# A wait that ties each group of GpSimd's operations to the VectorE instruction before it in the plan

## The chip, the cores and the metric

The kernel runs on one core of one Trainium2 chip. The core has five instruction streams that run side by side and meet only at semaphores: TensorE (PE), VectorE (DVE), ScalarE (ACT), GpSimd (POOL) and SyncE (SP), which only issues DMAs here. The metric is the device time of one execution in microseconds, the median of several.

## What is computed

Three blocks follow each other, for a batch of 8 sequences of 576 rows and 512 columns, all in float32:

```python
def sm_attn(qq, kk, vv):
    s = scale * np.matmul(qq, kk.transpose(0, 1, 3, 2))
    s = s - np.max(s, axis=-1, keepdims=True)
    a = np.exp(s)
    a = a / (np.sum(a, axis=-1, keepdims=True) + 1e-09)
    return np.matmul(a, vv)
p_packed = sm_attn(p, k, v)              # 32 packed rows for each head
out = sm_attn(q, p_packed, p_packed)     # 8 heads of 64
...
h = np.maximum(x @ w_in, 0.0)            # second block
u, v = (h[..., :d_ff // 2], h[..., d_ff // 2:])
v_n = (v - mu) / np.sqrt(var + 1e-06)
v_s = np.einsum('ts,bsd->btd', w_spatial, v_n) + b_spatial[None, :, None]
gated = u * v_s
return (gated @ w_out).astype(np.float32)
...
theta = x @ w_theta                      # third block
zr, zi = x * np.cos(theta), x * np.sin(theta)
y = np.einsum('ts,bsd->btd', w_tok_r, zr) + np.einsum('ts,bsd->btd', w_tok_i, zi)
u = x + y
return (u + np.maximum(u @ w_ch, 0.0)).astype(np.float32)
```

## The kernel before, in words

The matmuls run in fp32r, a float32 of shortened mantissa. To keep the precision, most operands are split into a high part and the rest: ScalarE writes the high part (`hi`, line 263) and VectorE or GpSimd subtracts it from the value (`lo`, line 266); a product is then three matmuls, high by high, high by low and low by high. These subtractions are the greater part of what GpSimd does. The rest is subtraction and multiplication in the softmax (lines 549 and 560), the products x cos and x sin in `rotate` (line 1226), differences of blocks in `TTop` (line 1392), and some sums of weight blocks.

No loop over tiles is written out in the order in which it runs. The source adds tasks to a planner (`Plan.add`): an engine or a choice of engines, an estimated duration, a function that emits the instructions, a due key, and what the task reads, writes and newly allocates. A task is one group of instructions on one engine. `Plan.run` then goes through time: of all ready tasks it takes the one that can start first, with a preference for the lowest key within 0.25 us, fixes its engine and its buffers, and emits it. So the order on each engine is the plan's order. A hand-tuned table (`SHIFT`) moves the keys of single tasks.

Tasks marked `port=True` are those of VectorE and GpSimd that work from SBUF to SBUF. The planner lets only one of these run at a time on the two engines together: the variable `port` is the end of the last one. That is a rule of the plan alone. In the program, an instruction waits for the data that it reads and for the buffers that it writes, by semaphores, and for nothing else (`manual_schedule`). Two instructions of VectorE and GpSimd that share no data may come in the other order, or at once.

The stages in time: up to about 330 us the eight batches pass through attention (`first`, `second` with its softmax in `second_quad`, tiles `t`, `sm`, `at`), the input matrix (`m_part`, `v_part`, `u_part`, tiles `vf`, `VN`, `VA`) and the spatial matmul (`g_part`, tile `gs`), while the weights of the third block are read, converted from 64-bit words (`cvt_tasks`, lines 705 to 714, tiles `raw`, `cvg`) and split. From about 330 us on come the products with the combined weights (`x_tile`, `x_pair`, tiles `WX`, `gp`, `xs`, `fa`), `rotate`, the splits into `op`, the token mixing (`product`, tiles `wg`, `WR`) in a scheme with sums and differences of blocks, the additions into `xs` (lines 1273, 1278), and the channel matmul (`chan`, line 1354) with the store of the result. `xs` and `fa` are the two results of a tile; `bank` is a PSUM bank.

Of the kernel before, what the change touches and what calls it, by code (L numbers as in the profile page):

```python
# [116 lines left out]
class Res:  # L117


    def __init__(self, t=None, pool=None):  # L120
        self.t, self.pool = t, pool
        self.before, self.writers, self.readers, self.left, self.end = [], [], [], 0, 0.0
# [36 lines left out]
class Plan:  # L159
# [5 lines left out]

    OVERLAP = {"DVE": 0.07, "ACT": 0.09}

    def __init__(self):
        self.tasks, self.pools = [], {}
        self.group = 0  # L170
        self.lag = 0.0
# [33 lines left out]
    def run(self):  # L205
        free = {}
        port = pipe = 0.0
        ready = [t for t in self.tasks if not t.wait]
        log = []
        n = len(self.tasks)  # L210
        while ready:
            by = {}
            for t in ready:
                s = self.start_of(t)
                if s is not None:
                    for e in t.choice:
                        by.setdefault(e, []).append((max(s, free.get(e, 0.0), port if t.port and e != "ACT" else 0.0), t))
            pick = None
            for e, c in by.items():
                m = min(s for s, _ in c)  # L220
                s, t = min(((s, t) for s, t in c if s <= m + self.SLACK), key=lambda x: (x[1].key, x[0]))
                if pick is None or s < pick[0]:
                    pick = s, t, e
            assert pick, "no buffer comes free"
            s, t, t.eng = pick
            t.dur = t.choice[t.eng]
            ready.remove(t)
            for x in t.new:
                p = self.pools[x.pool]
                best = min(range(len(p)), key=lambda i: p[i][0])  # L230
                x.t = p.pop(best)[1]
            free[t.eng] = s + t.dur - self.OVERLAP.get(t.eng, 0.0)
            end = s + t.dur
            if t.size:
                pipe = max(s + 0.3, pipe) + t.size / self.BYTES_PER_US
                end = pipe + 2.0
            if t.port and t.eng != "ACT":
                port = end
            t.fn(t.eng) if t.told else t.fn()
            n -= 1  # L240
            log.append((s, end, t))
            for x in t.res:
                x.left -= 1
                x.end = max(x.end, end)
                if not x.left and x.pool:
                    self.pools[x.pool].append((x.end, x.t))
            for u in t.users:
                u.ready = max(u.ready, end + ((0.0 if t.eng == "PE" else 0.05) if t.eng in u.choice and len(u.choice) == 1 else 0.3 if t.eng == "PE" else 0.2) + (u.lag if t.eng != "PE" else 0.0))
                u.wait -= 1
                if not u.wait:  # L250
                    ready.append(u)
        assert not n
        self.log = log


@with_exitstack
def moe_kernel(ctx: ExitStack, tc, qT, kT, v, pT, w_in, wsT, bs, w_out,
               w_theta, wrT, wiT, w_ch, out):
    nc = tc.nc
    V, A, G, PE, SP = nc.vector, nc.scalar, nc.gpsimd, nc.tensor, nc.sync  # L260

    def hi(out, in_):
        A.activation(out=out, in_=in_, func=AF.Copy)  # L263
# [69 lines left out]
    M = [apm.tile([128, 2, DFF], F32R, name=f"M{i}") for i in range(2)]  # L333
    AT = [apm.tile([128, 2, 640], F32R, name=f"at{i}") for i in range(2)]

    P = Plan()

    def tiles(pool, name, n, shape, dtype=F32):
        P.pool(name, [pool.tile(shape, dtype, name=f"{name}{i}") for i in range(n)])

# [44 lines left out]
    def load(key, dst, pairs, size, r=(), w=(), new=()):  # L385
        def fn():
            for o, i in pairs():
                SP.dma_start(out=o, in_=i)
        P.add("SP", 0.6 * len(pairs()) if not new else 0.6, fn, key, r=r, w=w, new=new, size=size)

# [13 lines left out]
    def rows(r):  # L404
        return slice(r * 64, r * 64 + 64)

    def logits(key, stat, stat_r, x, new, s, one):

        for quads in ((0,), (1,)) if one else ((0, 1),):
            def f(quads=quads):  # L410
                heads_mm(lambda q, c: s[q][c].t[:, :CH], lambda q, j, r: stat[rows(r), q, j * 32:j * 32 + 32],
                         lambda q, j, r, c: x[q].t[rows(r), j, c * CH:(c + 1) * CH], quads)
            P.add("PE", 1.0, f, key + 3 * quads[0], r=[y for q in quads for y in (stat_r[q], x[q])],
                  new=[y for q in quads for y in (*s[q], *new[q])])

    def banks(n):

        return [[P.res("bank") for _ in range(2)] for _ in range(n)]


    def first(b, key):
        kt, vr = ([P.res(n) for _ in range(2)] for n in ("kt", "vr"))
        s = banks(2)

        def load_p():
            SP.dma_start(out=pk[b % 2].rearrange("p q n -> p (q n)"), in_=pT[:, b * 128:(b + 1) * 128])
        P.add("SP", 0.6, load_p, key - 6.2, w=[R_pk[b % 2]], size=65e3)
        for q in range(2):
            def load_k(q=q):
                SP.dma_start(out=kt[q].t, in_=kT[b, q * 256:(q + 1) * 256, :].rearrange("(j p) t -> p j t", p=128))  # L430
            P.add("SP", 0.6, load_k, key - 6, new=[kt[q]], size=590e3)
        for q in range(2):
            def load_v(q=q):
                c = slice(q * 256, (q + 1) * 256)
                SP.dma_start(out=vr[q].t[:, 0:4, :], in_=v[b, 0:512, c].rearrange("(j p) t -> p j t", p=128))
                SP.dma_start(out=vr[q].t[0:64, 4, :], in_=v[b, 512:576, c])
            P.add("SP", 1.1, load_v, key - 4 + q, new=[vr[q]], size=590e3)
        logits(key, pk[b % 2], [R_pk[b % 2]] * 2, kt, [[], []], s, not b)
        for q in range(2):
            first_quad(b, q, key + 4 * q, s[q], vr[q])  # L440
# [565 lines left out]
    early = {*R_pk, *R_PP.values(), *R_win}  # L1006
    late = {*R_at.values(), *R_M.values()}
# [9 lines left out]
    made = {}  # L1017
# [546 lines left out]
```

## Time and profile before

| | us |
|---|---|
| median of 3 runs | 849.61 (848.97 to 850.67) |
| the profiled execution | 851.74 |
| its span, first to last instruction | 850.0 |
| PE busy in it | 833.3 |
| VectorE busy | 614.6 |
| ScalarE busy | 459.5 |
| GpSimd busy | 320.1 |

The busy time of an engine is the union of its instructions' times in the span. Ends of matmuls are modelled, so a busy PE is not PE at its peak. The 1.7 us between the profiled execution's time and its span lie before the first and after the last instruction. The mean granted clock of TensorE is 0.998 of full speed.

### The profile page before, as it was taken

The numbers are of one execution on the slowest core, as the hardware profiler recorded it, in microseconds if no ns is written. First come the engines' busy times: TensorE is split into PE (matmuls) and PEld (weight loads), VectorE is DVE, ScalarE is ACT, GpSimd is POOL, SyncE is SP. The second block draws the span as 40 slices with busy tenths as digits, with TensorE's granted clock in tenths as the row PEclk, the third lists the DMA queues.
The fourth block names the chain that finished last, engine by engine and source line by source line (L and its number), as shares of the span: only waits on it lengthen the run. The fifth ranks groups of instructions, "written<-read, shape, count | busy, mean of one in ns | idle before, by whom it ended". The sixth has DMA issues, their size and how long they took to land.

```text
span 850.0 us, 14886 instructions
## 1 busy us (share of the span) xinstructions
PE 833.3 (98%) x5526; PEld 690.4 (81%) x5526; DVE 614.6 (72%) x1187; ACT 459.5 (54%) x963; POOL 320.1 (38%) x243
## 2 busy tenths in 40 slices
PE   9999999999999999989999999999999999999998
PEld 7868888887787899868778888888887888888886
DVE  5999989888778983675985678775579675556333
ACT  4786856765675763673464564344553454534310
POOL 1312414233624043034256552515554221655520
PEclk9999999999999999999999999999999999999999
DMA  9986666647564239361133224142331343322621
GB/s 333 317 284 230 188 191 201 231 128 214 160 203 117 83 97 275 87 221 54 51 120 114 85 75 130 52 154 84 92 110 60 102 118 107 85 76 62 182 67 62
DMA packets 86860, 119.04 MB, mean 140 GB/s; under 512 B 10882, under 2 KB 57730, under 8 KB 86788
## 3 DMA queue, kind: packets, MB, share of 16 engines
q1 hardware_dynamic: 86788, 118.09, 44.4%
q8 instruction: 43, 0.70, 0.4%
q14 instruction: 29, 0.24, 0.1%
HBM read 88.38 MB, written 29.69 MB: 139 GB/s over the span
## 4 chain that ended last, share of the span: by engine, by line
PE 83%; DVE 11%; DMA 3%; ACT 1%; issue 1%; POOL 0%; SPq 0%; POOLq 0%; DVEq 0%; ACTq 0%
PE bank L269 80%; PE bank L1328 2%; DMA kt<-kT 1%; DMA raw<-wrT 1%; DVE fa L1226 1%; PE bank L461 1%; DVE op L266 1%; DVE fa L1392 1%; DMA vr<-vL 1%; DVE xs L1278 0%; DVE gp L266 0%; DVE sm L554 0%; DVE one L447 0%; DVE fa L1218 0%; DVE M L266 0%
## 5 line engine op out<-in xcount | busy, mean ns | idle before, releaser
L269 PE MATMUL bank<-op,wg 128*128 128x512 f32 x672 | 175.6, 395 | 1.0 <-DVE xs L1273 1.0
L269 PE MATMUL bank<-WX,gp 128*128 128x512 f32 x630 | 153.6, 391 | 2.0 <-ACT fa L1176 1.6
L269 PEld LDWEIGHTS bank<-op,wg 128*128 128x128 f32 x672 | 125.1, 189 | 26.9 <-DVE xs L1273 1.4
L269 PEld LDWEIGHTS bank<-WX,gp 128*128 128x128 f32 x630 | 117.7, 188 | 28.0 <-ACT fa L1176 2.5
L266 POOL TENSOR_TENSOR op<-fa,op 128x512 fp32r<-128x512 f32 x72 | 96.2, 1355 | 111.7 <-ACT op L263 109.8
L269 PE MATMUL bank<-WS,VN 128*128 128x288 f32 x768 | 116.4, 298 | 0.0
L269 PEld LDWEIGHTS bank<-WS,VN 128*128 128x128 f32 x768 | 105.8, 188 | 8.4 <-issue 4.5
L269 PE MATMUL bank<-WC,uT 128*128 128x512 f32 x432 | 103.9, 390 | 1.1 <-DVE xs L1354 1.1
L269 PEld LDWEIGHTS bank<-WC,uT 128*128 128x128 f32 x432 | 80.7, 188 | 18.1 <-DVE xs L1354 1.5
L1176 ACT ACTIVATE xs<-bank 128x256 f32<-128x256 f32 x60 | 22.9, 382 | 124.0 <-PE bank L269 118.0
L263 ACT ACTIVATE op<-fa 128x512 fp32r<-128x512 f32 x96 | 59.2, 630 | 55.0 <-PE bank L269 52.3
L1226 POOL TENSOR_TENSOR fa<-xs,fa 128x512 f32<-128x512 f32 x27 | 36.5, 1368 | 129.0 <-ACT fa L1222 103.9
L1273 DVE TENSOR_TENSOR xs<-bank,xs 128x512 f32<-128x512 f32 x56 | 37.9, 687 | 42.0 <-PE bank L269 41.9
L269 PE MATMUL bank<-M,at 128*128 128x512 f32 x240 | 59.6, 397 | 0.0
L1354 DVE SCALAR_TENSOR_TENSOR xs<-bank,xs 128x512 f32<-128x512 f32 (+1 forms) x37 | 24.9, 674 | 43.9 <-PE bank L269 43.8
L269 PE MATMUL bank<-at,M 128*128 128x288 f32 x384 | 54.6, 298 | 0.1
L269 PEld LDWEIGHTS bank<-at,M 128*128 128x128 f32 x384 | 52.1, 188 | 1.1 <-ACT ur L660 0.3
L269 PEld LDWEIGHTS bank<-M,at 128*128 128x128 f32 x240 | 43.7, 188 | 10.3 <-issue 0.9
L263 ACT ACTIVATE uT<-bank 128x512 fp32r<-128x512 f32 x36 | 21.2, 597 | 46.7 <-PE bank L269 24.9
L1180 DVE TENSOR_TENSOR xs<-bank,xs 128x256 f32<-128x256 f32 x45 | 18.9, 420 | 36.5 <-ACT xs L1176 18.1
L269 PE MATMUL bank<-op,WR 128*128 128x512 f32 x128 | 40.2, 395 | 3.2 <-DVE xs L1278 3.2
L266 POOL TENSOR_TENSOR VN<-vf,VN 128x512 fp32r<-128x512 f32 x13 | 18.7, 1452 | 52.8 <-ACT VN L263 52.8
(190 smaller groups left out, 1568.2 us busy)
## 6 DMA issues: line engine op xcount, KB each, us to landing
wg<-Wd SPq DMA_DIRECT2D x56, 512.0 KB, 3.7
kt<-kT SPq DMA_DIRECT2D x16, 576.0 KB, 5.5
q<-qT SPq DMA_DIRECT2D x16, 576.0 KB, 6.4
vr<-vL SPq DMA_DIRECT2D x16, 512.0 KB, 6.7
out<-xs SPq DMA_DIRECT2D x32, 256.0 KB, 2.0
g<-Gd SPq DMA_DIRECT2D x60, 128.0 KB, 2.8
Wd<-raw SPq DMA_DIRECT2D x56, 128.0 KB, 2.0
Gd<-gs SPq DMA_DIRECT2D x16, 288.0 KB, 3.2
```

Source lines behind the costliest of these rows:

```text
L263: A.activation(out=out, in_=in_, func=AF.Copy)
L266: (eng or V).tensor_tensor(out=out, in0=in_, in1=h, op=ALU.subtract)
L269: PE.matmul(out, lhsT, rhs, start=start, stop=stop, skip_group_check=more)
L461: PE.transpose(p1.t[:, k * 128:(k + 1) * 128], a1.t[:, k * 128:(k + 1) * 128], ident)
L1176: A.activation(out=to[a].t[:, c], in_=bank.t[:, a * 256:(a + 1) * 256], func=AF.Copy)
L1180: V.tensor_tensor(out=to[a].t[:, c], in0=bank.t[:, a * 256:(a + 1) * 256], in1=to[a].t[:, c], op=ALU.add)
L1226: P.add(TT, 0, lambda e, zf=zf: ENG[e].tensor_tensor(out=zf.t, in0=xs.t, in1=zf.t, op=ALU.mult), key + 0.3 + q, r=[xs, zf], w=[zf], port=True)
L1273: P.add("DVE", 0.69, lambda: V.tensor_tensor(out=xs.t, in0=ps.t, in1=xs.t, op=ALU.add), key - 8, r=[ps, xs], w=[xs])
L1328: PE.transpose(pt.t[:, d * 128:(d + 1) * 128], xs.t[:, d * 128:(d + 1) * 128], ident)
L1354: lambda c=c: V.scalar_tensor_tensor(out=xs.t[:, c], in0=ps.t[:, c], scalar=0.0, in1=xs.t[:, c], op0=ALU.max, op1=ALU.add), key + CC, r=[p ...
L1392: P.add(TT, 0, lambda e: ENG[e].tensor_tensor(out=out.t, in0=a.t, in1=b.t, op=ALU.subtract), key, r=[a, b], w=[] if new else [out], new=[o ...
```

## The change

`V` and `G`, the names by which the kernel calls VectorE and GpSimd, become thin wrappers that keep a list of the instructions that they make. `Plan.run` notes for each VectorE task its planned end and its last instruction. When it emits a GpSimd task that starts at `s` in the plan, it takes of the last 12 VectorE tasks those that end in the plan by `s + 0.1`, and makes the first instruction of the GpSimd task wait, by a semaphore, for the last instruction of the latest of them. Order, engines, buffers and all other waits stay.

```diff
-    def __init__(self):
+    def __init__(self, hold=None):
+        self.hold = hold
...
-        log = []
+        log, ends = [], []
+        made, hold = self.hold
...
+            if t.eng in ("POOL", "DVE"):
+                made[t.eng].made.clear()
             t.fn(t.eng) if t.told else t.fn()
+            if t.eng == "DVE":
+                ends.append((end, made["DVE"].made[-1]))
+            elif t.eng == "POOL" and made["POOL"].made:
+                before = [i for e, i in ends[-12:] if e <= s + 0.1]
+                if before:
+                    hold(made["POOL"].made[0], before[-1])
...
+class Recorder:
+    def __init__(self, eng):
+        self.eng, self.made = eng, []
+    def __getattr__(self, name):
+        f = getattr(self.eng, name)
+        if not callable(f):
+            return f
+        def call(*a, **k):
+            self.made.append(f(*a, **k))
+            return self.made[-1]
+        return call
...
-    V, A, G, PE, SP = nc.vector, nc.scalar, nc.gpsimd, nc.tensor, nc.sync
+    V, A, G, PE, SP = Recorder(nc.vector), nc.scalar, Recorder(nc.gpsimd), nc.tensor, nc.sync
...
-    P = Plan()
+    P = Plan(({"DVE": V, "POOL": G}, lambda late, early: tc.add_manual_dep(
+        late.ins if hasattr(late, "ins") else late, (early.ins if hasattr(early, "ins") else early).name,
+        mybir.DependencyInfo(mybir.DependencyClass.Sync, mybir.DependencyReason.DATA), reason="order of the shared port")))
```

## Rows read from the trace of the kernel before

**Rows 1.** The page: busy us (share of the span) by engine, and the last chain.

```profile
PE 833.3 (98%) x5526; PEld 690.4 (81%) x5526; DVE 614.6 (72%) x1187; ACT 459.5 (54%) x963; POOL 320.1 (38%) x243
...
PE 83%; DVE 11%; DMA 3%; ACT 1%; issue 1%; POOL 0%; SPq 0%; POOLq 0%; DVEq 0%; ACTq 0%
```

**Rows 2.** Stretches: length, busy us (instructions) of each engine, granted clock, DMA share, GB/s.

```profile
core 0: us, PE busy (x) PEld busy (x) DVE busy (x) ACT busy (x) POOL busy (x), PEclk, DMA share, GB/s
...
45.00:190.00 145.00, 143.30 (x1617) 120.54 (x1619) 129.20 (x323) 103.97 (x250) 44.51 (x32) 1.00 0.64 206
...
370.00:385.00 15.00, 11.83 (x46) 9.22 (x45) 14.56 (x16) 8.74 (x15) 3.43 (x2) 0.89 0.64 206
...
435.00:620.00 185.00, 185.00 (x839) 153.27 (x838) 123.13 (x196) 92.26 (x177) 92.38 (x69) 1.00 0.32 99
```

**Rows 3.** What PE waited for in the span: us in total, times, longest.

```profile
PE bank L269 <- DVE xs L1278: 3.2, 1, 3.2
PE bank L269 <- ACT fa L1176: 1.6, 2, 1.5
...
PE bank L269 <- DVE xs L1354: 1.1, 1, 1.1
PE bank L488 <- ACT pd L485: 1.0, 2, 0.7
PE bank L269 <- DVE xs L1273: 1.0, 1, 1.0
...
PE bank L1328 <- DVE fa L1180: 0.6, 1, 0.6
```

**Rows 4.** VectorE's groups of instructions: count, busy us, mean ns, idle before.

```profile
L1273 DVE TENSOR_TENSOR xs<-bank,xs 128x512 f32<-128x512 f32 x56 | 37.9, 687 | 42.0 <-PE bank L269 41.9
```

**Rows 5.** Timeline, 374 to 389 us: start, length, engine, instruction, count [idle before].

```profile
375.02 3.43 POOL L266 TENSOR_TENSOR op<-fa,op 128x512 fp32r<-128x512 f32 x2 [6.50 <-ACT op L263]
...
375.64 1.68 DVE L266 TENSOR_TENSOR op<-fa,op 128x512 fp32r<-128x512 f32 x1
...
377.24 2.30 DVE L266 TENSOR_TENSOR WX<-WX,WX 128x1024 fp32r<-128x1024 f32 x1
...
381.02 3.50 DVE L266 TENSOR_TENSOR WX<-WX,WX 128x1024 fp32r<-128x1024 f32 x3
...
385.73 3.57 PE L269 MATMUL bank<-WX,gp 128*128 128x512 f32 x15
```

**Rows 6.** Timeline of VectorE, 400 to 434 us.

```profile
400.22 0.43 DVE L1218 TENSOR_SCALAR fa<-fa 128x512 f32<-128x512 f32 x1 [1.36 <-ACT fa L1176]
...
405.17 1.51 DVE L1218 TENSOR_SCALAR fa<-fa 128x512 f32<-128x512 f32 x1
...
412.51 3.37 DVE L1392 TENSOR_TENSOR fa<-fa,tt 128x512 f32<-128x512 f32 x2
```

**Rows 7.** Timeline of VectorE, 626 to 643 us.

```profile
627.72 1.51 DVE L1218 TENSOR_SCALAR fa<-fa 128x512 f32<-128x512 f32 x1
```

**Rows 8.** Timeline of VectorE, GpSimd and PE, 200 to 233 us.

```profile
201.12 2.29 DVE L555 TENSOR_SCALAR sm<-sm 128x18 f32<-128x18 f32 x1
...
222.72 0.74 POOL L850 TENSOR_TENSOR raw<-cvg,cvg 128x256 f32<-128x256 f32 x1 [2.14 <-DVE cvg L714]
...
228.78 3.09 POOL L266 TENSOR_TENSOR at<-f,at 128x640 fp32r<-128x640 f32 x2
...
232.06 1.20 PE L269 MATMUL bank<-M,at 128*128 128x512 f32 x4
```

**Rows 9.** Timeline of GpSimd, 316 to 328 us.

```profile
319.17 5.92 POOL L266 TENSOR_TENSOR VN<-vf,VN 128x512 fp32r<-128x512 f32 x4 [12.07 <-ACT VN L263]
```

**Rows 10.** Timeline of VectorE, GpSimd and ScalarE, 61 to 67 us.

```profile
61.92 0.75 DVE L547 TENSOR_REDUCE sm<-t 128x18 f32<-128x576 f32 x1
...
62.81 1.16 POOL L549 TENSOR_TENSOR t<-t,sm 128x576 f32<-128x576 f32 x1 [0.38 <-DVE sm L547]
...
65.01 0.69 DVE L710 SCALAR_TENSOR_TENSOR raw<-raw 128x512 int32<-128x512 int32 x1
...
65.91 0.71 ACT L551 ACTIVATE t<-t 128x576 f32<-128x576 f32 x1
```

## The prediction

> **What bounds the kernel now.** I read the page first: TensorE (PE) is busy for 98% of the span, and the chain that ended last is PE for 83% and VectorE (DVE) for 11%; VectorE is busy for 614.6 us, GpSimd (POOL) for 320.1 of 850 [rows 1]. Then the stretches: from 435 to 620 us PE is busy for all of its 185 us, so nothing can be won there, and a late operand costs its full lateness; from 45 to 190 us PE lacks 1.7 us. From 370 to 385 us it lacks 3.2 us at a mean granted clock of 0.89 [rows 2]. Then what PE waited for: its long waits are few, and most are for VectorE or for a ScalarE (ACT) instruction behind VectorE [rows 3]. So VectorE matters in four places: 193 to 220, 374 to 385, 400 to 433 and 627 to 643 us. GpSimd is on the chain nearly nowhere.
>
> Last, the instructions in those places. A 128x512 VectorE addition that reads PSUM takes 687 ns, mean of 56, whatever GpSimd does [rows 4]. VectorE instructions with both inputs in SBUF take about as long when alone, but some take 1.4 to 2.3 us: those that start while a GpSimd instruction runs, and they end when it has ended. At 375.64 one took 1.68 us because GpSimd's pair had started at 375.02; the next, a 128x1024 one, took 2.30 us where three of its kind later took 3.50 together [rows 5]. The blocking goes both ways: that GpSimd pair took 3.43 us; two that are a quarter larger took 3.09 at 228.78, which makes 2.5 for a pair of this size, an estimate [rows 5, 8].
>
> **The change, part by part.** The wrapper around the two engines only remembers instructions; it issues none. What is added is one semaphore wait for the first instruction of each GpSimd group. There are 243 GpSimd instructions, 8 of them set-up, and the one `sums` group on GpSimd has four, so 232 groups. Nothing else is held: VectorE doesn't wait for GpSimd's turn, and the order on each engine is the same. Which VectorE instruction a group gets follows from the planner's order in the source. In a plan without lateness it has always ended; on the chip VectorE is often behind GpSimd, and there the wait bites.
>
> The wait itself: a GpSimd instruction that already waits for VectorE starts 0.14 us after it (sub at 62.81, after the row at 61.92 that ends at 62.67) [rows 10]. Each bound group pays that once, on an engine with 530 us idle [rows 1]; I take it as nothing beside the delays below. Behind the waiting instruction stands all later GpSimd work, and for it wait ScalarE (exp, padding), PE (op, at, VN, VA operands) and VectorE (a few differences).
>
> Gains, by place:
> A, 374 to 385 us. In the plan both split groups of 375.02 come after the WX instruction at 377.24, the second even after the last WX of the row at 381.02. Without them, VectorE's 1.68 becomes 0.68 and its 2.30 becomes 3.50/3 = 1.17 to 1.22: 2.08 us earlier, and PE's 3.2 us wait for xs L1278 shrinks to 1.1 [rows 3, 5]. The clock: 15 us at 0.89 is 1.65 us of PE work lost after that wait [rows 2]; a wait of 1.1 us may not cost it. What is late next is the last WX: PE's WX,gp row at 385.73 starts 1.2 us after it (381.02 + 3.50), so PE can win at most 2.08 + 1.2 = 3.3. Bounds 0 and 3.3; between 2.1 (the clock falls anyway) and 3.3 I take the middle, 2.7.
> B, 400 to 433 us. VectorE's L1218 took 1.51 instead of 0.43 as at 400.22 (the 1.08 is a GpSimd group that began at 404.72 and is planned after it); ScalarE and then PE wait behind it (1.6 us). Two L1392 took 3.37 instead of two times 0.69, with GpSimd groups that the plan puts after them [rows 4, 6]. PE's wait for xs L1273, 1.0, comes behind a pair of splits; of GpSimd's two splits there the plan puts one between them, so that collision stays in part. Bounds 0 and 2.6 [rows 3]; I take 1.1 + 0.6 = 1.7.
> C, 627 to 643 us. Four VectorE instructions are stretched by GpSimd groups that the plan has later, the first from 0.43 to 1.51 us; three later ones of the same pattern by 0.75 to 1.08, 3.9 in all [rows 6, 7]. The waits of PE behind them are 1.1 + 0.6 = 1.7 [rows 3], less than 3.9, so all of it: 1.7 (bounds 0 and 1.7).
> D, 193 to 220 us. VectorE's L555 took 2.29 us for 18 numbers a partition, behind a GpSimd group that the plan has behind it [rows 8]; VectorE's work before and after it feeds ScalarE, and PE's wait of 1.0 us for pd is behind ScalarE [rows 3]. Bounds 0 and 1.0; I take 0.7.
> Sum of gains 6.8.
>
> Losses, by place:
> E, 222 to 232 us. GpSimd's `sums` starts its first instruction, 0.74 us long, before VectorE's cvg L714 has ended; only its second one, at 222.72, waits for that today. With the wait the first goes there and all that follows without a gap ends some 0.8 later. The at pair ends at 231.87 and PE takes it at 232.06 [rows 8]: 0.6 lost.
> F, 319 to 327 us. Four VN groups in a row [rows 9] and VA after them; the second is held until a woT instruction of VectorE has ended, 0.7 us later than now. PE takes VA soon after it ends. Bounds 0 and 0.7; the middle, 0.4, lost.
> G, softmax, 17 to 280 us. The second subtraction of a quad is held behind weight conversion: the one of 62.81 would wait for L710, which ends at 65.70, so it would start at 65.84 and end 3.0 us later than now, at 67.0; its exp started at 65.91, so 1.1 us of it would be felt, less what VectorE wins back in front of L710 [rows 10]. The at operands that come of it were ready 0.2 us (E) or more before PE. Bounds 0 and, with 1.3 us in each of eight batches, 10. Nearest the row with 1.1, felt once, I take 1.0.
> After 435 us groups are held too. PE is never out of work from 435 to 620 us [rows 2], so its operands are ahead of it; by how much no one row tells, and VectorE wins back some of the time. Bounds 0 and 2, the size of the losses above; I put nothing.
> Sum of losses 2.0.
>
> Net 6.8 - 2.0 = 4.8: the profiled execution, 851.74 us (span 850.0, 1.7 around it, 0.25% above the median), would be 846.9, and the median 849.6 - 4.8 = 844.8.
>
> A rule is weighed here. All these rows show an instruction kept for the whole of another one, at 375.64 for 1.0 us, and the one from PSUM never [rows 4, 5]. The Trainium skill, SBUF — State Buffer, section Who interferes with whom, says this too, a lock held for the whole instruction, and adds that issue order decides who is blocked. By that, a GpSimd group let go at the end of one VectorE instruction loses the lock to the next one, which the trace agrees with (3.43 us for two where 2.5 would do). It is a rival below, with its own sum: 847.6 instead of 844.8.
>
> **Rivals.**
> 1. GpSimd loses each race (chance 0.12). VectorE starts its next instruction at once, GpSimd 0.14 us after the wait ends, so a held group is blocked by one more two-input instruction, about 0.7 us. For it: the pair of 3.43 us. Against: many next instructions read PSUM (687 ns, unmoved). Price: 4 groups in a row, as in E, 2.8 more: 847.6.
> 2. The gains don't arrive (0.17). The collision moves to VectorE's next instruction, as many are stretched one after the other in C, and PE waits as before; or the wait is implied already and nothing changes. Against: at A nothing collides after the held pair but instructions that read PSUM. Time 849.6, give or take 1.
> 3. Slower (0.15): softmax late. One mechanism: the subtraction and product groups of `second_quad` on GpSimd get tied to conversion work that VectorE does in between; exp, sum and product follow each other over three engines, so each of eight batches loses 1.3 us at PE, which has nothing to give there [rows 2, 10]. It decides from 6.8 us of loss on. 10 - 6.8 = 3.2 slower: 852.8.
> 4. All gains and few losses (0.08): A to D at their upper bounds are 8.6, with no loss: 841.0.
> My forecast: 0.48.
>
> **How the numbers follow.** A measurement of this kernel can tell about 0.2%, 1.7 us, from no change. Faster: the forecast, rival 4 and two thirds of rival 1, 0.64. Same: rival 2 and part of rival 1 and 3, 0.21. Slower: 0.15. The forecast's own range is 842.3 (losses 0, G and F wrong, A at its top) to 847.5 (A at 2.1, B at 0.6, D at 0). The range that holds 8 in 10 leaves out rival 3's upper part and the best of rival 4: 840.8 to 850.6.
>
> **What would show it.** Right: PE's wait for xs L1278 near 378 us is 1.1 us or less and the granted clock from 370 to 385 us is near 1.00; VectorE's busy time falls from 614.6 us while GpSimd's waits name VectorE; the waits behind fa L1176, xs L1354 and fa L1180 are gone; PE gets new waits for at near 230 and VA near 325 us, each under 1 us. Wrong: PE waits before v_part's at operands of more than 1 us in several batches, VectorE instructions as long as before, or op operands that come late after 435 us, where PE has no idle time.

## The result, and the profile after

The changed kernel takes 838.33 us, median of 5 runs (837.67 to 840.70), against 849.61 for the kernel before. The ratio is 0.9867 (95% interval 0.9849 to 0.9886): 11.3 us faster, with bounds of 9.7 and 12.8. Forecast were 844.8 us and a range of 840.8 to 850.6. The sign was right; the gain is more than twice the forecast, and the time lies below the range. The profiled execution took 838.33 us as well, its span is 836.5.

The order of the instructions on every engine is the same as before. In this trace all VectorE and GpSimd instructions carry the line of the wrapper, L278, so they are told apart by their tiles; the other lines have moved by 27 to 29 (L269 is now L296, L1176 is L1205). The page's busy times and its last chain, against [rows 1]:

```profile
PE 827.7 (99%) x5526; PEld 688.4 (82%) x5526; DVE 584.9 (70%) x1187; ACT 462.4 (55%) x963; POOL 305.7 (37%) x243
...
PE 93%; DVE 3%; DMA 3%; ACT 0%; issue 0%; SPq 0%; ACTq 0%
```

VectorE is busy 29.7 us less and GpSimd 14.4 us less, with the same instructions. VectorE's share of the last chain falls from 11% to 3%. Three stretches (the columns are those of [rows 2]):

```profile
45.00:190.00 145.00, 144.31 (x1648) 121.00 (x1646) 128.30 (x324) 104.93 (x251) 42.42 (x33) 1.00 0.65 206
370.00:385.00 15.00, 15.00 (x67) 11.97 (x66) 10.93 (x15) 7.81 (x13) 5.48 (x5) 1.00 0.43 133
435.00:620.00 185.00, 185.00 (x845) 153.27 (x844) 117.39 (x199) 92.49 (x176) 85.95 (x68) 1.00 0.34 101
```

From 370 to 385 us PE has no gap left and the granted clock is 1.00, full speed, where it was 0.89. From 435 to 620 us PE was full before and is full now; GpSimd's delay there costs nothing. What PE still waits for, against [rows 3]:

```profile
PE bank L296 <- POOL ident masks.py:199: 1.4, 1, 1.4
PE bank L296 <- DMA q<-qT: 1.3, 1, 1.3
PE bank L517 <- ACT pd L514: 0.7, 2, 0.5
PE bank L296 <- ACT fa L1205: 0.6, 2, 0.4
PE bank L296 <- ACT aT L496: 0.5, 1, 0.5
PE bank L804 <- DVE gs L278: 0.4, 1, 0.4
PE bank L296 <- DVE xs L278: 0.2, 1, 0.2
```

All waits of 1 us or more behind VectorE are gone, and the one behind GpSimd's `VA` is not in the list.

Where the time came from can be read by following the same matmul rows through both traces. First PE's timeline of the kernel before (start, length, engine, instruction, count; the row at 385.73 stands in [rows 5]):

```profile
199.19 1.22 PE L269 MATMUL bank<-WS,VN 128*128 128x288 f32 x8
...
220.13 1.86 PE L269 MATMUL bank<-WS,VN 128*128 128x288 f32 x12
...
376.81 1.06 PE L269 MATMUL bank<-op,wg 128*128 128x512 f32 x3
...
381.04 0.78 PE L269 MATMUL bank<-op,WR 128*128 128x512 f32 x2 [3.17 <-DVE xs L1278]
...
433.05 3.25 PE L269 MATMUL bank<-op,wg 128*128 128x512 f32 x13 [1.00 <-DVE xs L1273]
...
642.65 2.56 PE L269 MATMUL bank<-WC,uT 128*128 128x512 f32 x10 [1.05 <-DVE xs L1354]
```

And the same rows of the changed kernel:

```profile
198.59 1.23 PE L296 MATMUL bank<-WS,VN 128*128 128x288 f32 x8
...
217.71 1.76 PE L296 MATMUL bank<-WS,VN 128*128 128x288 f32 x12
...
373.20 0.95 PE L296 MATMUL bank<-op,wg 128*128 128x512 f32 x3
...
374.04 0.73 PE L296 MATMUL bank<-op,WR 128*128 128x512 f32 x2
...
377.30 5.62 PE L296 MATMUL bank<-WX,gp 128*128 128x512 f32 x24
...
422.11 4.16 PE L296 MATMUL bank<-op,wg 128*128 128x512 f32 x17 [0.24 <-DVE xs L278]
...
629.49 2.90 PE L296 MATMUL bank<-WC,uT 128*128 128x512 f32 x12
```

The lead is 0.60, 2.42, 3.61, then 7.00 (381.04 to 374.04), 8.43 (385.73 to 377.30), 10.94 and 13.16 us, and 13.5 at the end of the spans. So D gave 1.8, A 4.8, B 2.5 and C 2.2, together 11.3. Of A's 4.8, 3.4 are the wait that is gone and 1.4 the matmuls behind it, which ran partly at the lower clock before. The other 2.1 us (0.6 before 199 us, 1.2 between 220 and 377, 0.3 at the end) are about what the profiled execution of before lay above its median, 851.74 - 849.61. Most of the 1.2 is shown below to be no part of the change. These prices are those of one execution of each kernel, and that of before had at A the longest wait seen there and the lower clock behind it; the experiments say how far they hold in the mean.

### The profile page after: what moved, and what is told of

It is laid out like the page before. It is cut to its first block, busy times and chain, and to the rows that moved or that the text cites. A ratio compares the mean times of both kernels' runs of the same rounds, so it can differ in the third digit from the quotient of the medians.

```text
span 836.5 us, 14912 instructions
## 1 busy us (share of the span) xinstructions
PE 827.7 (99%) x5526; PEld 688.4 (82%) x5526; DVE 584.9 (70%) x1187; ACT 462.4 (55%) x963; POOL 305.7 (37%) x243
## 4 chain that ended last, share of the span: by engine, by line
PE 93%; DVE 3%; DMA 3%; ACT 0%; issue 0%; SPq 0%; ACTq 0%
PE bank L296 90%; DMA q<-qT 2%; PE bank L1357 2%; DVE fa L278 1%; PE bank L490 1%; DMA kt<-kT 1%; DVE gp L278 0%; DVE sm L278 0%; DVE xs L278 0%; DVE M L278 0%; PE bank L517 0%; DVE op L278 0%; PE bank L804 0%; DVE f L278 0%; PE bank L491 0%
## 5 line engine op out<-in xcount | busy, mean ns | idle before, releaser
L296 PE MATMUL bank<-op,wg 128*128 128x512 f32 x672 | 174.4, 393 | 0.2 <-DVE xs L278 0.2
L296 PE MATMUL bank<-WX,gp 128*128 128x512 f32 x630 | 153.1, 390 | 0.6 <-ACT fa L1205 0.6
L296 PEld LDWEIGHTS bank<-op,wg 128*128 128x128 f32 x672 | 124.2, 188 | 25.8 <-DVE xs L278 0.7
L296 PEld LDWEIGHTS bank<-WX,gp 128*128 128x128 f32 x630 | 117.8, 188 | 25.9 <-ACT fa L1205 1.4
L278 DVE TENSOR_TENSOR xs<-bank,xs 128x512 f32<-128x512 f32 (+2 forms) x125 | 73.3, 592 | 92.0 <-PE bank L296 70.0
L278 POOL TENSOR_TENSOR op<-fa,op 128x512 fp32r<-128x512 f32 x72 | 93.5, 1315 | 107.3 <-ACT op L290 61.7
L296 PE MATMUL bank<-WS,VN 128*128 128x288 f32 x768 | 116.2, 298 | 0.0
L296 PEld LDWEIGHTS bank<-WS,VN 128*128 128x128 f32 x768 | 105.8, 188 | 8.3 <-issue 5.4
L296 PE MATMUL bank<-WC,uT 128*128 128x512 f32 x432 | 103.8, 390 | 0.0
L296 PEld LDWEIGHTS bank<-WC,uT 128*128 128x128 f32 x432 | 80.8, 188 | 16.7
L1205 ACT ACTIVATE xs<-bank 128x256 f32<-128x256 f32 x60 | 23.0, 383 | 118.1 <-PE bank L296 112.1
L278 POOL TENSOR_TENSOR fa<-xs,fa 128x512 f32<-128x512 f32 x27 | 34.6, 1294 | 114.9 <-ACT fa L1251 47.9
L278 POOL TENSOR_TENSOR t<-t,sm 128x576 f32<-128x576 f32 x27 | 31.3, 1161 | 88.7 <-DVE sm L278 37.6
L296 PE MATMUL bank<-M,at 128*128 128x512 f32 x240 | 59.6, 397 | 0.0
L278 DVE SCALAR_TENSOR_TENSOR xs<-bank,xs 128x512 f32<-128x512 f32 (+1 forms) x37 | 24.9, 675 | 48.2 <-PE bank L296 48.2
L296 PE MATMUL bank<-at,M 128*128 128x288 f32 x384 | 54.3, 297 | 0.0
L296 PEld LDWEIGHTS bank<-at,M 128*128 128x128 f32 x384 | 52.0, 188 | 0.8 <-ACT aT L496 0.2
L296 PEld LDWEIGHTS bank<-M,at 128*128 128x128 f32 x240 | 43.7, 188 | 10.3 <-issue 1.3
L296 PE MATMUL bank<-op,WR 128*128 128x512 f32 x128 | 39.7, 391 | 0.0
L278 POOL TENSOR_TENSOR fa<-fa,fa 128x512 f32<-128x512 f32 x24 | 31.0, 1294 | 19.2 <-DVE fa L278 8.9
```

The lines of the kernel that those rows point to most:

```text
L278: self.made.append(f(*a, **k))
L296: PE.matmul(out, lhsT, rhs, start=start, stop=stop, skip_group_check=more)
L1205: A.activation(out=to[a].t[:, c], in_=bank.t[:, a * 256:(a + 1) * 256], func=AF.Copy)
```

## The experiments

None leaves out any of the work; each is the changed kernel with the edit shown, cut to the lines that differ. Ratios are to the kernel before on the same chip. Its median was 850.75 us beside the runs with all the places, with all but these, with A alone and with the first edit of `t.port`; 849.54 us beside D alone, B and C alone, `t.port` with waits both ways, and the change again; 850.59 us beside the other four. The ratios are those of the means of the executions within 0.0005, not of the medians, and a gain is given as its share of 849.6 us. By medians most gains are within 1 us of that; where the difference matters it is said.

**Only the places A to D, and all but these.**

```diff
-                if before:
+                if before and any(a <= s <= b for a, b in ((188, 254), (365, 376), (395, 430), (610, 645))):
```

> The hold only for groups of GpSimd planned in 188-254, 365-376, 395-430 and 610-645 us (the places A to D, with E). Theory 'local': the time is won only where TensorE waited behind a VectorE instruction that GpSimd had blocked, so nearly the whole gain of the change is here: 838.3 to 839.3. Rival 'losses were there': the holds of VN and of the softmax (terms F and G, 1.4 us) cost what was predicted and were covered by larger gains; without them 836.9. Rival 'spread': the 14 us that GpSimd and the 30 us that VectorE are less busy help everywhere; then 843 to 846.

840.47 us, ratio 0.9889 (0.9867 to 0.9910), 9.4 us won. Most of the change's gain lies in these places. Leaving out the holds of F and G made nothing faster: "losses were there" falls, and "spread" too. What is lacking against the change (9.4 against 11.3, with intervals that overlap) is partly one new wait just behind the last held group. VectorE, GpSimd and PE there:

```profile
427.37 1.73 DVE L278 TENSOR_TENSOR fa<-fa,fa 128x512 f32<-128x512 f32 x1
...
427.26 2.98 POOL L278 TENSOR_TENSOR op<-fa,op 128x512 fp32r<-128x512 f32 x2 [3.19 <-ACT op L290]
...
429.76 1.42 PE L296 MATMUL bank<-op,wg 128*128 128x512 f32 x5 [0.36 <-DVE xs L278]
```

A GpSimd pair that is no longer held starts 0.11 us ahead of a VectorE product, which takes 1.73 us and not 0.69, and PE waits (0.36 us; PE's lead falls by 0.6 there). This is the mechanism of the whole case in three rows.

The complement has `not` in front of `any`.

> The hold for all groups but those of the run before (softmax of six batches, the VN splits, all of 435 to 610 us and the end). Local: no gain but the 0.6 us before 190 us, 848.5 to 849.6. Losses were there: 851.0. Spread: 843 to 846.

846.13 us, ratio 0.9966 (0.9948 to 0.9984), 2.9 us won (1.4 to 4.4); 4.6 between the medians. "Local" had no more than 1.1 here, so it falls in its strict form. Rows of ScalarE, VectorE, GpSimd and PE of this run:

```profile
330.36 0.63 ACT L290 ACTIVATE op<-op 128x512 fp32r<-128x512 f32 x1 [9.52 <-DMA op<-Gd]
...
372.55 0.69 DVE L278 TENSOR_TENSOR op<-fa,op 128x512 fp32r<-128x512 f32 x1
...
372.57 4.06 POOL L278 TENSOR_TENSOR op<-fa,op 128x512 fp32r<-128x512 f32 x2 [6.42 <-PE bank L296]
...
376.98 0.73 PE L296 MATMUL bank<-op,WR 128*128 128x512 f32 x2 [0.88 <-DVE xs L278]
```

The gain is at A, though A's groups are not held. ScalarE's `op` work ahead of it starts behind a load (`op<-Gd`) at 330.36, 3.3 us earlier than in the trace of before (333.67), while PE leads by 1.7 only (VectorE's `cvg` addition, which waits for PE, goes from 331.70 to 330.04). VectorE comes to the `op` split at 372.55 and GpSimd to its pair at 372.57: now VectorE is first, by 0.02 us, its split takes 0.69 us, and GpSimd is the one that is blocked (4.06 us for the pair). PE's wait of 3.2 [rows 3] is down to 0.9. So A can be won by a lead from upstream as well as by a hold. Mean and median lie apart because three of the twelve executions took 848.1 to 851.7 us, at a mean granted clock of 0.996 or 0.997, and nine 844.8 to 847.8 us at 0.999 or 1.000. That the race was lost in the three would fit; no trace of them is there.

**Single places.**

```diff
-                if before:
+                if before and 365 <= s <= 376:
```

> The hold for the two split groups at 375 us alone. Local, priced by the two traces (wait of 3.4 us gone and 1.4 us of half clock behind it): 849.6 - 4.8 = 844.8. By the prediction's upper bound, WX late next: 846.3; by its value: 846.9. If the lead is given back at the next late operand of VectorE near 400 us: 849.

846.46 us, ratio 0.9962 (0.9949 to 0.9975): 3.2 us won (2.1 to 4.3); 4.3 between the medians. Its trace shows the upper price. PE's timeline:

```profile
199.10 1.22 PE L296 MATMUL bank<-WS,VN 128*128 128x288 f32 x8
...
375.48 0.95 PE L296 MATMUL bank<-op,wg 128*128 128x512 f32 x3
376.61 0.73 PE L296 MATMUL bank<-op,WR 128*128 128x512 f32 x2 [0.19 <-DVE xs L278]
...
379.69 1.52 PE L296 MATMUL bank<-WX,gp 128*128 128x512 f32 x6
```

Its lead grows from 1.33 (376.81 to 375.48) to 6.04 us (385.73 to 379.69), so 4.7 at A. Nothing is held between 199.10 and 375.48, yet the lead goes from 0.09 to 1.33: the 1.2 us of that stretch belong to the execution of before that was profiled. That the mean gain is less than 4.7 fits a price of A that differs from execution to execution (last section).

```diff
-                if before:
+                if before and 188 <= s <= 254:
```

> The hold for groups planned in 188 to 254 us alone (place D, with E behind it). Local, by the two traces: the waits for pd (0.9) and VA (0.7) and the rest of D go, 1.9 us: against a kernel before of 850.6 that is 848.7. By the prediction, 0.7 won at D and 0.6 lost at E: no change, 850.5. If this lead of 1.9 us is eaten at the next late operand: no change either.

847.08 us, ratio 0.9973 (0.9961 to 0.9984): 2.3 us won, 1.4 to 3.3. The 1.9 of the local theory is inside, the 0.7 of the prediction is not, and E, which is held here too, costs nothing that shows.

```diff
-                if before:
+                if before and (395 <= s <= 430 or 610 <= s <= 645):
```

> The hold for groups planned in 395 to 430 and 610 to 645 us alone (places B and C). Local, by the two traces: 2.5 + 2.5 = 5.0 faster, 845.6 against a kernel before of 850.6. By the prediction's values, 1.7 + 1.7: 847.2. If B or C needs the lead won at A: 847 to 848.

845.31 us, ratio 0.9948 (0.9933 to 0.9963): 4.4 us won, 3.1 to 5.7; the prediction's 3.4 is inside, the 4.7 of the two traces nearer. B and C need no lead from A.

```diff
-                if before:
+                if before and 350 <= s < 365:
```

> The hold for the four rotate groups of 358 to 369 us alone, ahead of place A; the two split groups of A itself aren't held. Theory 'upstream': the additions of A are late also because L1218 and L1219 at 366 to 369 us were blocked for 1.6 us, and a VectorE that is earlier by 1.4 us takes the port ahead of the split group by itself; then the wait at A shrinks by 2.4 us and the half clock behind it (1.0) goes: 3.4 faster than before, 846.5. If only the collision inside A counts, as the prediction had it: no change, 849.6 to 850.7.

850.30 us, ratio 0.9996 (0.9983 to 1.0008). The theory "upstream" in this form falls. VectorE's rows:

```profile
366.55 0.69 DVE L278 TENSOR_TENSOR fa<-fa,fa 128x512 f32<-128x512 f32 x1
369.23 0.69 DVE L278 TENSOR_TENSOR op<-fa,op 128x512 fp32r<-128x512 f32 x1 [1.98 <-ACT op L290]
...
374.78 1.68 DVE L278 TENSOR_TENSOR op<-fa,op 128x512 fp32r<-128x512 f32 x1
```

The product L1219 is no longer blocked (0.69 us), but VectorE then waits 1.98 us for ScalarE, longer by what was won, and the collision at A is as it was. Here a stretched instruction ahead of a wait for another engine cost nothing. It also shows that the wrapper with a few holds changes nothing by itself.

**What must a group wait for?**

```diff
-                ends.append((end, made["DVE"].made[-1]))
+                if t.port:
+                    ends.append((end, made["DVE"].made[-1]))
```

> The hold behind the last VectorE task that works from SBUF to SBUF (port=True) instead of the last one of any kind; a group then no longer waits for additions that read PSUM. Order at the shared port is the cause: as the change, 838.3 within 0.8, with VectorE busy near 585 us. If it is GpSimd's lateness in general that helps (125 groups were ahead of their partner, 66 of them behind a PSUM instruction): between, about 843.

837.75 us, ratio 0.9859 (0.9834 to 0.9883); VectorE busy 578.8, GpSimd 303.8 us. Waiting behind the instructions that read PSUM adds nothing: it is the order of SBUF-to-SBUF work that counts. This is the fastest median of all, but its interval takes in the change's ratio of 0.9867.

```diff
-                if before:
-                    hold(made["POOL"].made[0], before[-1])
+                if len(before) > 1:
+                    hold(made["POOL"].made[0], before[-2])
```

> Each group waits for the last but one VectorE task instead of the last one. Theory 'rough order': released 0.14 us after that task ends, GpSimd finds VectorE's next task already running and is itself the one that is blocked, so VectorE keeps most of its gain: 838 to 840, with GpSimd's own time up by some 5 to 10 us. Rival 'exact': the one-task lead is enough for GpSimd to take the port first about half of the time: 843 or more, VectorE busy near 600 us.

840.34 us, ratio 0.9877 (0.9856 to 0.9898), 10.5 us won.

```profile
PE 828.7 (99%) x5526; PEld 688.6 (82%) x5526; DVE 590.6 (70%) x1187; ACT 461.2 (55%) x963; POOL 316.9 (38%) x243
```

GpSimd is busy 11 us longer than in the change, VectorE 6: released one task early, GpSimd is itself blocked more often. "Rough order" holds, "exact" falls.

```diff
+                if t.port:
+                    before = [i for e, i in held[-4:] if e <= s + 0.1]
+                    if before:
+                        hold(made["DVE"].made[0], before[-1])
...
+                held.append((end, made["POOL"].made[-1]))
```

> The change, and VectorE tasks from SBUF to SBUF also wait for the GpSimd group that ends last ahead of them in the plan. VectorE's stretched time (22 us in the changed kernel) falls below 5 us. If that still sets TensorE's last waits (2.4 us in all, 1.2 of them behind VectorE): 837.0 to 838. If VectorE now waits out late GpSimd groups instead: VectorE's idle time grows by more than its busy time falls and PE pays for it, 840 to 845.

839.51 us, ratio 0.9866 (0.9847 to 0.9886). VectorE's busy time falls by 17 us more and nothing comes of it: its waits behind GpSimd, 1.2 us in sum in the change, are 34.9 us here. The page's busy times, and the longest row of the list of these waits (us in total, times, longest):

```profile
PE 828.1 (99%) x5526; PEld 688.2 (82%) x5526; DVE 568.1 (68%) x1187; ACT 461.1 (55%) x963; POOL 303.7 (36%) x243
```

```profile
DVE fa L283 <- POOL op L283: 7.4, 6, 2.3
```

The same, with the edit of the run with `t.port` added on GpSimd's side:

> Waits both ways, each only behind the last SBUF-to-SBUF task of the other engine. If VectorE's added waits cost as much as the stretched time that they save, as in the run with waits both ways: 838 to 839.5. If that run's time came of GpSimd waiting behind PSUM instructions: 836.5 to 837.5.

839.16 us, ratio 0.9875 (0.9859 to 0.9891): again no better than the change.

```diff
-                before = [i for e, i in ends[-12:] if e <= s + 0.1]
+                before = [i for e, i in ends[-12:] if e <= s + 1.5]
```

> The change with a tolerance of 1.5 us instead of 0.1: a group also waits for a VectorE task that overlaps it in the plan. If the losses were nil because GpSimd's results are ready well before they are used: 838.3 within 1. If they are just hidden, each group 0.7 us later brings them out (E, F, G, 2 us): 840 to 841.

843.29 us, ratio 0.9911 (0.9892 to 0.9931): a third of the gain is lost, more than either theory said. A row of GpSimd and one of PE:

```profile
71.21 1.16 POOL L278 TENSOR_TENSOR t<-t,sm 128x576 f32<-128x576 f32 x1 [1.68 <-DVE f L278]
...
72.97 0.33 PE L517 MATMUL bank<-ident,pd 128*128 128x128 f32 x1 [1.02 <-ACT pd L514]
```

This is of the kind of G: a product of the softmax is held on GpSimd for 1.7 us behind a VectorE transposition, ScalarE's work comes late behind it, and at 72.97 PE waits 1.0 us for ScalarE. (Another wait of 1.1 us, at 417.42, is for VectorE's `gp`.) So a hold that goes further than the plan's order does make losses of the kind that the forecast feared.

**The change again**, beside the last runs:

> The changed kernel again, beside the others on one chip: 838.3 within 1, the sum of A (4.3 to 4.8), B and C (5.0) and D (1.9) below a kernel before of 849.6 to 850.6. If the parts don't add up, the sum of the single runs differs from it by more than 1.5 us.

838.50 us, ratio 0.9871 (0.9852 to 0.9889), 11.0 us won. The single places sum to 3.2 + 4.4 + 2.3 = 9.9 us, all four in one kernel gave 9.4, the rest alone 2.9, by its trace most of it A's a second time. They add up within the intervals.

## Why the prediction was wrong in size

**Right: the mechanism and the places.** VectorE instructions that GpSimd had blocked were ahead of PE's long waits, at the four places named, and the hold takes these waits away. "The gains don't arrive" (rival 2) and the late softmax (rival 3) did not come, and of the signs named the new waits for `at` and `VA` stayed away. Rival 1, that GpSimd loses each race, fell too: the rows of its splits in the changed kernel show it mostly unblocked.

```profile
L278 POOL TENSOR_TENSOR op<-fa,op 128x512 fp32r<-128x512 f32 x72 | 93.5, 1315 | 107.3 <-ACT op L290 61.7 <-PE bank L296 21.5 <-DVE fa L278 11.1
```

1315 ns is the mean of 72 (1355 before); the pair of [rows 5] took 3430 together. The Trainium skill, SBUF — State Buffer, section Who interferes with whom, has the lock go to the one that issues first, for the whole instruction; the two races above, won by 0.02 us by VectorE and by 0.11 us by GpSimd, agree.

**The step that failed first: "Sum of losses 2.0".** It measured as nothing. F and G, and E in part, were worked out with the partner's end as the trace of before had it. But the partner, VectorE's instruction, ends earlier once nothing blocks it and its predecessors. G's own example, the subtraction of 62.81, in the changed kernel (VectorE's L710, GpSimd, ScalarE):

```profile
63.54 0.69 DVE L278 SCALAR_TENSOR_TENSOR raw<-raw 128x512 int32<-128x512 int32 x1
...
64.38 1.16 POOL L278 TENSOR_TENSOR t<-t,sm 128x576 f32<-128x576 f32 x1 [2.29 <-DVE raw L278]
...
65.58 0.71 ACT L580 ACTIVATE t<-t 128x576 f32<-128x576 f32 x1
```

L710 starts at 63.54 and not at 65.01, the subtraction ends at 65.54 and not at 67.0, and the exp starts at 65.58, 0.33 us earlier than before [rows 10]. PE's lead is no more than 0.6 up to 199 us, so 0.3 at most is felt where 1.1 was forecast. E and F, GpSimd's rows and PE's `at` row:

```profile
219.08 0.74 POOL L278 TENSOR_TENSOR raw<-cvg 128x256 f32<-128x256 f32 x1 [3.01 <-issue]
...
225.84 3.09 POOL L278 TENSOR_TENSOR at<-f,at 128x640 fp32r<-128x640 f32 x2
...
317.26 3.79 POOL L278 TENSOR_TENSOR VN<-vf,VN 128x512 fp32r<-128x512 f32 x3 [0.46 <-DVE woT L278]
...
229.54 2.81 PE L296 MATMUL bank<-M,at 128*128 128x512 f32 x11
```

The `sums` group is held as forecast (219.08, only 0.76 us ahead of where it was, while PE leads by 2.4), but the `at` pair ends at 228.93, 2.94 us earlier than before [rows 8], and PE takes it without a wait. `VN` is held at 317.26 for 0.46 us, but three splits then take 3.79 us, unblocked, and the row ends at 321.05, 4.0 us earlier than before [rows 9], where PE leads by 3.6.

At E the prediction also read too little slack. The run with D alone shows it, for there the delay did come: GpSimd's pair and PE's row.

```profile
228.09 3.07 POOL L278 TENSOR_TENSOR at<-f,at 128x640 fp32r<-128x640 f32 x2
...
230.62 1.65 PE L296 MATMUL bank<-M,at 128*128 128x512 f32 x6
```

The pair ends at 231.16, 0.7 us earlier than before, where PE leads by 1.4; so it is 0.7 us late, as forecast. PE starts its row 0.5 us before that end and loses nothing. The source tells why: each product begins with the high part, and the second of the pair is needed first by the sixth weight load, 1.0 us into the row. The slack in the trace of before was therefore 1.2 us, and not the 0.2 from 231.87 to 232.06.

**The sum of gains, 6.8, measured as 11.3.** A: 4.8 where 2.7 stood, above its upper bound of 3.3. "What is late next is the last WX" was false. PE's WX,gp row starts at 377.30 while VectorE's last three WX subtractions run:

```profile
370.61 0.69 DVE L278 TENSOR_TENSOR op<-fa,op 128x512 fp32r<-128x512 f32 x1
371.22 1.22 DVE L278 TENSOR_TENSOR WX<-WX,WX 128x1024 fp32r<-128x1024 f32 x1
...
374.02 3.50 DVE L278 TENSOR_TENSOR WX<-WX,WX 128x1024 fp32r<-128x1024 f32 x3
```

They end at 377.52. And VectorE comes to A 5.03 us earlier than in the trace of before (375.64 to 370.61) where PE leads by 3.6: 1.4 us of lead from upstream on top of the 2.08 that I had counted (1.68 to 0.69 and 2.30 to 1.22, both as forecast). So all of the 3.2 us wait went, and the clock's 1.4 us behind it. Part of this was luck: in the run with A alone, where nothing upstream is held, VectorE comes to A at 373.28, 2.36 us earlier where PE leads by 1.33, so 1.0 us of such a lead is there without the change, and in the runs with D or with B and C alone it is 0.7 and 0.4. In the mean, A alone gave 3.2 us (2.1 to 4.3), an interval that holds the forecast 2.7.
D: 1.8 where 0.7 stood; its upper bound of 1.0 counted PE's wait for pd and left out its wait for `VA` (0.5 us), also in this stage, which went as well. B and C: 2.5 and 2.2 where 1.7 and 1.7 stood. At B the bound was right and I took too little of it; C's bound of 1.7 was the idle time of the waits, and PE's rows show 0.5 us more between their starts.

With gains of 11.3 and losses of 0 the sum is 849.6 - 11.3 = 838.3, the time measured; that it fits to 0.1 us is chance, since A's price differs between executions. By the runs on single places, of the gains only D's lies clear of the value forecast, and no run at the plan's own order shows the losses. Two ends of the forecast's own range were added up wrongly: by its terms they are 842.2 and 847.2, not 842.3 and 847.5. Rival 4, all gains and no losses, was the nearest to what happened; I gave it 0.08, and its 841.0 rested on the same too low bounds.

## What to carry to other kernels

Where two engines block each other at a shared port, the order of their instructions at that port is part of the schedule: a semaphore that keeps the planned order cost little here, and it needed only to stand behind the other engine's SBUF-to-SBUF work. When such a wait is priced, the instruction waited for must be moved forward too, since it is no longer blocked; a price taken at its old end is too high. The slack behind it is to be read at the first matmul that uses the late operand, not at the start of the row that it is part of. A hold beyond the plan's order, here by 1.5 us, gave back a third of the gain, and holds on both sides brought nothing more.

## What the runs showed of the hardware

The clock did not follow the length of the wait at A. In the run with B and C alone PE waited 2.9 us there, in the run with D alone 2.6 us; the rows of 370 to 385 us, first with B and C held, then with D:

```profile
370.00:385.00 15.00, 12.09 (x55) 9.70 (x54) 14.61 (x18) 7.55 (x12) 3.44 (x2) 1.00 0.53 174
```

```profile
370.00:385.00 15.00, 12.45 (x49) 9.76 (x49) 13.97 (x16) 6.76 (x11) 3.44 (x2) 0.89 0.42 145
```

After the longer wait the granted clock stayed at 1.00 (2.4 GHz), after the shorter one it fell for a time to half (0.50 from 379 to 381 us, 1.2 GHz), as it did after 3.2 us in the kernel before; in the runs with a wait of 0.9 us or less at A it stayed at 1.00 there. So the clock's part of A's gain is there in some executions and not in others. Of the 17 executions of the kernel before beside the last four runs, the eight with a mean granted clock of 0.999 or 1.000 took 847.9 to 849.5 us, the nine below that 849.3 to 851.8. That, and the wait at A itself (2.6 to 3.2 us in the kernel before and in the runs with D, with B and C, and with upstream alone), would explain that A's mean gain alone is below its gain in the traces; it is not shown by itself.

The change does not keep the clock up everywhere. In the profiled execution of the change again, at 841.33 us the slowest of its five, the granted clock was 0.51 from 47.00 to 50.50 us, in the attention stage, after PE waits of 1.07 and 0.91 us with 0.68 us of matmuls between them. What decides whether the clock falls was not tried, nor was the lead from upstream at A taken away by itself.
